# Block-sparse attention and a gated convolution feed-forward on one core: output turned on TensorE, one band exponential, gathers divided anew

## The chip, the cores and the metric

One core of one Trainium2 chip. The metric is the device time of one execution in microseconds. TensorE multiplies into PSUM; VectorE (DVE), ScalarE (ACT) and GpSimd (POOL) compute; SyncE (SP), ScalarE and POOL issue transfers. Each engine works through its own queue in order and waits on semaphores for the others.

## The reference

`q`, `k`, `v` have 4 batches, 8 heads, 768 positions and 64 channels. Blocks are of 32 positions, 24 in all. A query block sees its neighbours at distance at most 1, the first and the last block, and three sampled blocks from a table; the first and the last query block see everything.

```
scores = where(mask, q @ k.T / 8, -1e9);  attn = softmax(scores) @ v
x = attn with the heads side by side               # 4 x 768 x 512
h = relu(x @ w_in)                                 # 512 -> 1024
c = conv over positions, 3 taps per channel, of h
out = (h * sigmoid(c)) @ w_out                     # 1024 -> 512, float32
```

## The kernel before

**The planner.** The kernel does not issue its work in the order of the source. Each operation is entered with its engines and planned durations, its dependencies, the buffers that it takes or uses, and a due time; `Plan.run` (six passes and forty shaken trials) searches for an order of issue by list scheduling, and the instructions are then written out in that order, engine by engine. A planned duration or a dependency changes the order, never the data. The planner knows two transfer rings (POOL's, and one for all the others), a switch cost on TensorE, and buffers by pool. It knows nothing of how instructions reach an engine.

**The work.** There are 4 batches, 8 half-batches `n` (12 query blocks each), and in each of these 4 head pairs `hp`: 32 units of attention.
- Keys and queries: POOL loads a pair with a cast (L578), TensorE turns it (L606), ScalarE or VectorE evicts it as `kt` (L614, L616) and `qb` (L629, L631). POOL copies the keys of the first and last block into `kd` (L639, 64x64 tiles).
- Values: POOL loads half a batch (L656) into the one staging tile `vst`, POOL rearranges it (L669), SP writes it to a table `vs` in HBM (L677) and loads it back as `vn` (L684); POOL copies a version shifted by 64 rows (L692, two copies a batch), and SP loads the values of the first and last block as `vd` (L699, four small loads a batch).
- Sampled keys: VectorE copies 3 blocks for each of 11 query blocks out of `kt` at offsets read from registers (L740, 33 copies a half).
- Sampled values: the 11 blocks of a half are gathered out of `vs` into one of two `vg` buffers: `NIX` of them by indirect DMAs on POOL (L746; 4 in the first half, then 6), the others by SP with three transfers each (L755; in the first half three blocks by ScalarE).
- A unit of attention: band scores (L812, 11 matmuls), global scores (L841, L846), sampled scores (L864), each into one of two PSUM tiles `st`; the exponentials. That of the band is two instructions with a bias tile that holds -30000 in the rows outside the window (L821, 384 columns, and L822, 320 columns); the others are one each (L853, L871). A small memset zeroes one corner (L829, L831). The value product (L908, 67 matmuls) adds it all up, VectorE divides by the sum (L919, L920) into `xtok`, one of three, and SP turns that by a crossbar transpose into `xT` (L926).
- Feed-forward of a half: eight groups of four matmuls (L1062) that wait for the half's four `xT`, relu to `hE` (L1073 on ScalarE, L1075 on VectorE), then the convolution in four chunks of 256 channels. Chunks in `PEC` = (1, 3) run on TensorE with diagonal weights (L1023, six matmuls into an `st` tile); the others on VectorE (L976, six taps; L983, two adds). Then tanh (L991, L1032), a multiply (L1003, L1038), and the output product (L946), evicted (L954, L956) and stored by SP.

What sets the order around the change: the in-order queues of SP (value gathers, table writes, crossbar transposes, stores) and POOL (loads, copies, indirect gathers), the two `st` and four `mix` tiles of PSUM, and the planner's durations, such as `op({"POOL": 1.25}, ...)` for an indirect gather, `op({"DVE": 0.36}, cp, ...)` for three key copies and `op({"PE": 0.72}, a_fn, ...)` for a value product.

Of the kernel before, what the change touches and what calls it, by code (L numbers as in the profile page):

```python
# [52 lines left out]
class Op:  # L53
    __slots__ = ("alts", "fn", "prio", "deps", "lat", "dma", "mode", "allocs", "uses", "earliest", "outs",
                 "pend", "ready", "start", "end", "eng", "key", "done", "seq", "after", "lazy")
# [11 lines left out]
LAZY = 12.0  # L67


class Plan:  # L70
# [11 lines left out]
    def op(self, alts, fn, prio, deps=(), lat=None, dma=None, mode=None, alloc=(), uses=(), earliest=0.0,  # L82
           after=(), lazy=False):
        o = Op(alts, fn, prio, [d for d in deps if d is not None], lat, dma, mode, earliest)
        o.key = len(self.ops)
        o.lazy = lazy
        o.after = [d for d in after if d is not None]
# [22 lines left out]
    def forward(self, prio, first=True):  # L110
# [6 lines left out]
        rings = [0.0, 0.0]  # L117
        for o in ops:
# [12 lines left out]
        while left:  # L131
# [53 lines left out]
            if o.mode is not None:  # L185
                mode["PE"] = o.mode
            if o.dma is not None:
# [116 lines left out]
def kernel(  # L304
# [23 lines left out]
    PEC = (1, 3)  # L328
# [14 lines left out]
    NPA, NPR, NPG, NXK, NXT, NHE, NCV, NGT, NOS = 3, 3, 3, 3, 2, 2, 2, 2, 3  # L343
# [9 lines left out]
    vst = many(1, [96, 4, 8, 64], BF16, "vst")  # L353
# [20 lines left out]
    bias_f = sb.tile([128, 1], FP32, tag="bias_f", name="bias_f")  # L374
    bias_s = sb.tile([128, 1], FP32, tag="bias_s", name="bias_s")
# [17 lines left out]
    P_kg, P_vg, P_vn, P_vst, P_vr = pl.pool(NKG), pl.pool(NVG), pl.pool(NVN), pl.pool(1), pl.pool(1)  # L393
# [63 lines left out]
    def biases(e):  # L457
        nc.vector.memset(bias_f, 0.0)
        nc.vector.memset(bias_s, 0.0)
        nc.vector.memset(bias_f[96:128], -30000.0)  # L460
        nc.vector.memset(bias_s[0:32], -30000.0)
        nc.vector.memset(zrow, 0.0)
    bias_op = op({"DVE": 0.6}, biases, -7)
# [69 lines left out]
    for b in range(B):  # L533
        vs_zero.append(sp(lambda e, b=b: nc.sync.dma_start(out=vs_t[b][S:S + 32, :], in_=zrow), 4 + 8 * b, [bias_op],
                          0.1))
# [24 lines left out]
    def qk_load(P, x):  # L560
# [16 lines left out]
        else:  # L577
# [3 lines left out]
                after=[last_ld[0]], lazy=b > 0)  # L581
# [3 lines left out]
    def qk_pair(P):  # L585
# [9 lines left out]
        for x in range(2):  # L595
# [12 lines left out]
            trp = op({"PE": 0.42}, tr, due - 4 + 0.5 * x, [ld, i_sel, qm] + kt_w[b][:1], mode="T", alloc=[mb], uses=[nb])  # L608
            if x == 0:
# [7 lines left out]
                kt_w[b].append(op({"ACT": 0.70, "DVE": 0.62}, ev, due - 3, [trp] + kt_w[b][:1] + z_ops,  # L617
                                  uses=[mb, kt_buf[b]]))
                kev = kt_w[b][-1]
            else:  # L620
                qb_w[P] = []
                for h in range(2):
# [9 lines left out]
                    qb_w[P].append(op({"ACT": 0.70, "DVE": 0.62}, ev, due - 2.5, [trp, qm] + (qz[P:P + 1] if P < NQB else []),  # L632
# [15 lines left out]
    def v_batch(b):  # L648
        due = TS(8 * b)
        early = 0.0 if b == 0 else max(0.0, due - 26)  # L650
# [3 lines left out]
        for hf in range(2):  # L654
# [5 lines left out]
                dma=2.4, earliest=early, after=[last_v[0]], lazy=b > 0, uses=[] if nb else [he_first])  # L660
# [9 lines left out]
            alts = {"DVE": 0.75} if b == 0 else {"POOL": 2.3}  # L670
# [4 lines left out]
        for r in range(4):  # L675
# [8 lines left out]
        vn_w[b] = sp(lambda e: nc.sync.dma_start(  # L684
            out=VN[vn_buf[b].index], in_=vs_t[b][0:S].rearrange("(c p) e -> p c e", p=128)),
            due - 5, wr + [vm], 2.7, uses=[vn_buf[b]])
        vs_w[b] = []
        for h in range(2):
# [4 lines left out]
            vs_w[b].append(op({"DVE": 0.85} if b == 0 else {"POOL": 2.8}, sh, due - 3, [vn_w[b]], uses=[vn_buf[b]]))  # L693
        vd_w[b] = []
        for h in range(2):
            for x in range(2):
                def ldd(e, h=h, x=x):
                    rows = vs_t[b][(S - 32) * x:(S - 32) * x + 32, :].rearrange("p (a h d) -> p a h d", h=2, d=65)
                    nc.sync.dma_start(out=VD[vn_buf[b].index][64 * h + 32 * x:64 * h + 32 * x + 32, :,  # L699
                                                              65 * h:65 * h + 65], in_=rows[:, :, h, :])  # L700
# [451 lines left out]
```

## Time and profile before

| what | us |
|---|---|
| median of 3 runs | 319.02 |
| lowest, highest | 316.77, 325.29 |
| the profiled execution | 314.24 |
| its span from first to last instruction | 312.5 |

The profile is of one execution. Busy times are unions over an engine; a wait that names issue is time in which an engine waited for nothing that the profile shows. Line numbers are those of the kernel.

### The profile page before, as it was taken

What the parts mean: (1) busy time and instruction counts of PE and PEld (TensorE: products, weight loads), DVE (VectorE), ACT (ScalarE), POOL (GpSimd) and SP (SyncE); (2) the same over time, 40 slices, a digit from 0 to 9 for tenths busy, and PEclk for the clock granted to TensorE, in tenths of its full rate; (3) what the DMA queues carried; (4) which work ended last, traced back from release to release, by engine and by line L of the source; (5) the groups of instructions that cost most, each with busy time, mean ns of one, the idle gap of its engine ahead of it and who ended that gap; (6) DMA issues with size and microseconds to landing.
All of it is one profiled execution on the core that took longest, in us unless ns stands there. A gap on an engine that the chain in (4) does not pass through costs nothing.

```text
span 312.5 us, 10688 instructions
## 1 busy us (share of the span) xinstructions
PE 219.5 (70%) x4233; PEld 147.0 (47%) x4233; DVE 178.0 (57%) x652; ACT 162.0 (52%) x269; POOL 117.4 (38%) x170
## 2 busy tenths in 40 slices
PE   0744258659788293577895948997936577999994
PEld 0433147546445152366562635665624346676441
DVE  7725283027669682112685794744939246647781
ACT  2251255526557272336582853667823165966662
POOL 8157506910517388600066188305256600000000
PEclk9999999659999788958998697999985769999999
DMA  7987855990648924980379637965472431131013
GB/s 143 162 178 213 152 123 95 187 180 5 91 120 198 207 60 129 168 153 15 94 137 171 146 87 166 148 166 96 103 208 53 100 119 30 49 117 40 15 68 134
DMA packets 45542, 37.71 MB, mean 121 GB/s; under 512 B 19772, under 2 KB 40052, under 8 KB 45492
## 3 DMA queue, kind: packets, MB, share of 16 engines
q0 software_dynamic: 13216, 15.74, 29.5%
q1 hardware_dynamic: 31436, 20.59, 27.5%
q10 hardware_dynamic: 840, 0.70, 0.8%
q8 instruction: 33, 0.54, 0.8%
q14 instruction: 17, 0.14, 0.1%
HBM read 35.38 MB, written 9.62 MB: 144 GB/s over the span
## 4 chain that ended last, share of the span: by engine, by line
PE 46%; issue 14%; ACT 11%; DVE 10%; another core or an unknown queue 4%; DMA 2%; DVEq 1%; SPq 0%; ACTq 0%
PE mix L946 11%; PE mix L1062 11%; PE mix L908 9%; PE st L864 3%; DVE kg L740 3%; PE st L846 2%; ACT pr L871 2%; PE st L812 2%; PE st L1023 2%; PE mix L606 2%; ACT pg L853 2%; PE st L841 2%; ACT qb L629 2%; DMA vg<-vs 2%
## 5 line engine op out<-in xcount | busy, mean ns | idle before, releaser
L946 PE MATMUL mix<-woutb,gT 128*128 128x512 bf16 x192 | 53.6, 407 | 2.5 <-DVE gT L1038 1.2
L740 DVE COPY kg<-kt 128x128 bf16 x264 | 52.9, 241 | 3.7 <-issue 1.4
L746 POOL DMA_INDIRECT vg<-vs,idx x46 | 44.6, 969 | 22.9 <-issue 12.5
L1062 PE MATMUL mix<-xT,winb 128*128 128x384 bf16 x256 | 50.0, 345 | 1.7 <-DVE kt L616 1.3
L871 ACT ACTIVATE pr<-st 128x704 bf16<-128x704 f32 x32 | 24.2, 756 | 26.7 <-PE st L864 23.3
L812 PE MATMUL st<-qb,kt 128*128 128x64 bf16 x352 | 20.0, 210 | 23.7 <-issue 15.5
L853 ACT ACTIVATE pg<-st 128x736 bf16<-128x736 f32 x32 | 25.1, 785 | 21.5 <-PE st L846 9.9
L1062 PEld LDWEIGHTS <-winb 128*128 128x128 bf16 x256 | 25.5, 103 | 19.5 <-issue 6.0
L1073 ACT ACTIVATE hE<-mix 128x384 bf16<-128x384 f32 x53 | 25.8, 493 | 15.5 <-PE mix L1062 14.2
L908 PE MATMUL mix<-vg,pr 96*32 96x65 bf16 x704 | 28.4, 203 | 5.5 <-issue 5.5
L812 PEld LDWEIGHTS <-kt 128*128 128x128 bf16 x352 | 17.2, 109 | 28.7 <-issue 25.7
L606 PE MATMUL mix<-ident,nat 96*64 96x96 bf16 x512 | 18.4, 232 | 17.2 <-ACT kt L614 6.3
L578 POOL DMA_DIRECT2D nat<-in_k_dram x15 | 9.9, 665 | 54.4 <-PE mix L606 54.4
L908 PE MATMUL mix<-vn,pa 128*32 128x65 bf16 x384 | 25.5, 204 | 6.3 <-issue 6.3
L976 DVE TENSOR_SCALAR m<-hE,cw 128x384 bf16<-128x384 bf16 x96 | 23.7, 316 | 10.1 <-ACT hE L1073 10.1
L919 DVE RECIPROCAL rcp<-mix 128x6 f32<-128x6 f32 x32 | 6.2, 194 | 39.9 <-PE mix L908 39.8
L908 PE MATMUL mix<-vs,pa 128*32 128x65 bf16 x320 | 27.1, 203 | 2.6 <-issue 2.5
L908 PEld LDWEIGHTS <-pg 128*32 128x32 bf16 x736 | 23.5, 101 | 11.5 <-issue 11.4
L908 PE MATMUL mix<-vd,pg 128*32 128x130 bf16 x352 | 25.8, 234 | 2.8 <-issue 2.8
L908 PEld LDWEIGHTS <-pa 128*32 128x32 bf16 x704 | 22.0, 99 | 11.1 <-issue 10.8
L946 PEld LDWEIGHTS <-gT 128*128 128x128 bf16 x192 | 17.6, 103 | 19.9 <-issue 3.3
L864 PE MATMUL st<-qb,kg 128*128 128x64 bf16 x352 | 20.0, 210 | 9.1 <-ACT pa L822 6.2
(102 smaller groups left out, 433.7 us busy)
## 6 DMA issues: line engine op xcount, KB each, us to landing
out_dram<-o2s SPq DMA_DIRECT2D x24, 256.0 KB
vg<-vs SPq DMA_DIRECT2D x117, 32.5 KB
vn<-vs SPq DMA_DIRECT2D x4, 780.0 KB
nat<-in_k_dram POOLq DMA_DIRECT2D x15, 192.0 KB
nat<-in_q_dram POOLq DMA_DIRECT2D x15, 192.0 KB
vs<-vr SPq DMA_DIRECT2D x14, 195.0 KB
vst<-in_v_dram POOLq DMA_DIRECT2D x7, 384.0 KB
winb<-in_moe_w_in_dram POOLq DMA_DIRECT2D x1, 1024.0 KB
```

The lines of the kernel that those rows point to most:

```text
L606: nc.tensor.transpose(out=tp[64 * h:64 * h + 64, 96 * c:96 * c + 96], in_=nat[:, h, c, :], identity=ident[0:96, 0:96])
L740: nc.vector.tensor_copy(out=dst[:, :, x, 32 * s:32 * s + 32], in_=KT[kt_buf[b].index][:, :, bass.ds(block_off("DVE", i0 + x, s), 32)])
L746: vg_w[n].append(op({"POOL": 1.25}, lambda e, x=x: nc.gpsimd.indirect_dma_start(out=VG[vg_buf[n].index][:, x, :], out_offset=None, in_=vs_ ...
L812: nc.tensor.matmul(out=st[:, o + 64 * w:o + 64 * w + 64].rearrange("p (h s) -> p h s", h=2), lhsT=kt()[:, win(i):win(i) + 128], rhs=qcol(i ...
L853: nc.scalar.activation(out=pg_t[pg.index], in_=st_t[sg.index][:, 0:736], func=AF.Exp, bias=0.0, scale=0.125)
L864: nc.tensor.matmul(out=st[:, 64 * x:64 * x + 64].rearrange("p (h s) -> p h s", h=2), lhsT=kg[:, o:o + 128], rhs=qcol(i), start=True, stop= ...
L871: nc.scalar.activation(out=pr_t[pr.index], in_=st_t[sr.index][:, 0:704], func=AF.Exp, bias=0.0, scale=0.125)
L908: nc.tensor.matmul(out=dst, lhsT=l_, rhs=r_, start=(y == 0), stop=(y == len(lists[j]) - 1), skip_group_check=True)
L946: nc.tensor.matmul(out=mix_t[mb.index], lhsT=gT_t[gt_buf[n].index][:, ffc, 128 * c:128 * c + 128], rhs=woutb[:, ffc, :], start=(ffc == 0), ...
L976: nc.vector.tensor_scalar(out=mv(dst)[:, y], in0=hE_t[heb.index][:, f0 + y, c0 + tp_:c0 + tp_ + cn], scalar1=cw[:, tp_, f0 + y:f0 + y + 1] ...
L1062: nc.tensor.matmul(out=mix_t[hb.index][:, 0:384], lhsT=winb[:, fc, 128 * ffc:128 * ffc + 128], rhs=xT_t[xt_buf[n].index][:, fc, :], start= ...
L1073: nc.scalar.activation(out=dst, in_=src, func=AF.Relu, bias=0.0, scale=0.5)
```

## The change

- The output of a unit is turned by three TensorE transposes into a `mix` tile and evicted by ScalarE or VectorE into `xT`; the crossbar transposes go. `xtok` has two buffers and not three.
- The band is one exponential of 704 columns without a bias. The columns are ordered so that the blocks whose first 32 rows lie outside the window come first; these rows are zeroed by one memset of 32x384 behind the exponential (on VectorE or POOL), and the blocks at odd places multiply 96 rows, not 128.
- Indirect gathers: 4 in every half; the other 7 blocks by SP. Of the key copies 3 blocks in 11 (9 copies a half) go to POOL, with registers of its own.
- The convolution has one chunk on TensorE, `PEC` = (2,).
- The planner counts TensorE's instructions (`n`) and does not let an operation enter a page of 256 sooner than 2.3 us after the page before it was entered. Many planned durations are new.
- Values: staging in two buffers, no earliest time, rearranged by POOL or VectorE; `vn` loaded in halves; `vd` copied on the chip from `vn`. Two early query loads wait for writes of the value table; the weights are loaded in halves.

```diff
+PAGE, FETCH = 256, 2.3
...
+                        if o.n:
+                            g = (count + o.n) // PAGE
+                            if g != count // PAGE and s < pages.get(g, 0.0):
+                                s = pages[g]
...
+            if o.n:
+                g = (count + o.n) // PAGE
+                if g != count // PAGE:
+                    pages[g + 1] = o.end + FETCH
+                count += o.n
...
-    PEC = (1, 3)
+    PEC = (2,)
...
-    NPA, NPR, NPG, NXK, NXT, NHE, NCV, NGT, NOS = 3, 3, 3, 3, 2, 2, 2, 2, 3
+    NPA, NPR, NPG, NXK, NXT, NHE, NCV, NGT, NOS = 3, 3, 3, 2, 2, 2, 2, 2, 3
+    NVT = 2
...
-    vst = many(1, [96, 4, 8, 64], BF16, "vst")
+    vst = many(NVT, [96, 4, 8, 64], BF16, "vst")
...
-        early = 0.0 if b == 0 else max(0.0, due - 26)
+        early = 0.0
...
-                dma=2.4, earliest=early, after=[last_v[0]], lazy=b > 0, uses=[] if nb else [he_first])
+                dma=2.4, earliest=early, after=[last_v[0]], uses=[] if nb else [he_first])
...
-            alts = {"DVE": 0.75} if b == 0 else {"POOL": 2.3}
+            alts = {"DVE": 0.75} if b == 0 else {"POOL": 1.9, "DVE": 0.75}
...
-        vn_w[b] = sp(lambda e: nc.sync.dma_start(
-            out=VN[vn_buf[b].index], in_=vs_t[b][0:S].rearrange("(c p) e -> p c e", p=128)),
-            due - 5, wr + [vm], 2.7, uses=[vn_buf[b]])
+        vn_w[b] = []
+        for y in range(2):
+            vn_w[b].append(sp(lambda e, y=y: nc.sync.dma_start(
+                out=VN[vn_buf[b].index][:, 3 * y:3 * y + 3],
+                in_=vs_t[b][384 * y:384 * y + 384].rearrange("(c p) e -> p c e", p=128)),
+                due - 5, wr + [vm], 1.4, uses=[vn_buf[b]]))
...
-                    nc.sync.dma_start(out=VD[vn_buf[b].index][64 * h + 32 * x:64 * h + 32 * x + 32, :,
-                                                              65 * h:65 * h + 65], in_=rows[:, :, h, :])
-                vd_w[b].append(sp(ldd, due - 4.8, wr + [vm] + vz, 0.2, uses=[vn_buf[b]]))
+                    eng = nc.vector if e == "DVE" else nc.gpsimd
+                    src = VN[vn_buf[b].index][96 * x:96 * x + 32, 5 * x].rearrange("p (a h d) -> p a h d", h=2, d=65)
+                    r0 = 64 * h + 32 * x
+                    eng.tensor_copy(out=VD[vn_buf[b].index][r0:r0 + 32, :, 65 * h:65 * h + 65], in_=src[:, :, h, :])
+                vd_w[b].append(op({"DVE": 0.25, "POOL": 0.45}, ldd, due - 3, vn_w[b][x:x + 1] + vz, uses=[vn_buf[b]]))
...
-    NIX = [4] + [6] * (NHALF - 1)
+    NIX = [4] + [4] * (NHALF - 1)
...
+    KPX = 3
...
+            en = "POOL" if x >= NX - KPX else "DVE"
...
-            kg_w[n].append(op({"DVE": 0.36}, cp, due - 3 + 0.2 * x, [regs_d[g], km] + kt_w[b] + kgz,
+            kg_w[n].append(op({en: 0.55 if en == "DVE" else 0.95}, cp, due - 3 + 0.2 * x, [regs_p[g] if en == "POOL" else regs_d[g], km] + kt_w[b] + kgz,
                               uses=[kg_buf[n], kt_buf[b]]))
...
-            vg_w[n].append(op({en: 1.25}, gd, due - 3 + 0.5 * (x - NIX[n]), [regs_a if en == "ACT" else regs_s[g], vm]
+            vg_w[n].append(op({en: 1.75} if en == "SP" else {en: 2.1}, gd, due - 3 + 0.5 * (x - NIX[n]), [regs_a if en == "ACT" else regs_s[g], vm]
                               + vs_rows[b], dma=0.33, uses=[vg_buf[n]]))
...
-            nc.scalar.activation(out=p_[:, 0:384], in_=st[:, 0:384], func=AF.Exp, bias=b6, scale=0.125)
-            nc.scalar.activation(out=p_[:, 384:704], in_=st[:, 512:832], func=AF.Exp, bias=b5, scale=0.125)
-        ea = op({"ACT": t_act(384) + t_act(320)}, e_a, due, [so, bias_op], alloc=[pa], uses=[sa], lat=0.35)
+            nc.scalar.activation(out=pa_t[pa.index], in_=st_t[sa.index][:, 0:704], func=AF.Exp, bias=0.0, scale=0.125)
+        ea = op({"ACT": t_act(704)}, e_a, due, [so], alloc=[pa], uses=[sa], lat=0.35)
...
-            if g == 0:
-                eng.memset(p_[0:32, 0:64], 0.0)
-            else:
+            eng.memset(p_[0:32, 0:384], 0.0)
+            if g == 1:
                 eng.memset(p_[96:128, 320:384], 0.0)
-        fx = op({"POOL": 0.12, "DVE": 0.09}, fix, due + 0.5, [ea], uses=[pa])
+        fx = op({"DVE": 0.2 + 0.07 * g, "POOL": 0.45 + 0.1 * g}, fix, due + 0.5, [ea], uses=[pa])
...
-        xtr[(n, hp)] = sp(lambda e: nc.sync.dma_start_transpose(
-            out=xT_t[xt_buf[n].index][:, hp].rearrange("p (c s) -> p c s", c=3),
-            in_=xtok_t[xk.index].rearrange("p c h d -> p (c h d)")), due + 4.4, [no, xtr[(n, -1)]], 0.6, dur=1.27,
-            uses=[xk, xt_buf[n]])
+        xb = Buf(P_mix)
+
+        def xt(e):
+            tp = mix_t[xb.index].bitcast(BF16)
+            for c in range(3):
+                nc.tensor.transpose(out=tp[:, 128 * c:128 * c + 128],
+                                    in_=xtok_t[xk.index][:, c].rearrange("p h d -> p (h d)"), identity=ident)
+        xo = op({"PE": 0.19}, xt, due + 4.4, [no], mode="F", alloc=[xb], uses=[xk], n=6)
+
+        def xe(e):
+            src, dst = mix_t[xb.index].bitcast(BF16)[:, 0:384], xT_t[xt_buf[n].index][:, hp]
...
+        xtr[(n, hp)] = op({"ACT": 0.42, "DVE": 0.33}, xe, due + 4.8, [xo, xtr[(n, -1)]], uses=[xb, xt_buf[n]])
```

## Rows read from the trace of the kernel before

**Rows 1.** The page, part 1: busy us (share of the span) xinstructions.
```profile
PE 219.5 (70%) x4233; PEld 147.0 (47%) x4233; DVE 178.0 (57%) x652; ACT 162.0 (52%) x269; POOL 117.4 (38%) x170
```
**Rows 2.** Windows: length, busy us (x count) of PE, PEld, DVE, ACT, POOL; clock, DMA.
```profile
226.60:232.70 6.10, 1.28 (x7) 0.60 (x7) 1.88 (x11) 1.78 (x3) 3.74 (x5) 0.91 0.84 247
...
sum 37.10, PE 4.00 PEld 1.76 DVE 10.62 ACT 6.29 POOL 22.20; mean PE 0.67 PEld 0.29 DVE 1.77 ACT 1.05 POOL 3.70
```
**Rows 3.** Timeline of POOL: first and last of a train of six (start us, us).
```profile
163.11 1.19 POOL L746 DMA_INDIRECT vg<-vs,idx  x1 [0.30 <-issue]
...
169.69 0.92 POOL L746 DMA_INDIRECT vg<-vs,idx  x1 [0.30 <-issue]
```
**Rows 4.** Windows (columns as in rows 2), then SP's timeline, for one stretch.
```profile
42.70:53.10 10.40, 7.99 (x315) 6.92 (x318) 5.42 (x22) 7.33 (x13) 3.46 (x6) 1.00 0.38 64
...
42.73 10.38 SPq L755 DMA_DIRECT2D vg<-vs  x15
```
**Rows 5.** Queue of instructions (page, part 3), a window, pieces of the chain.
```profile
q8 instruction: 33, 0.54, 0.8%
...
66.20:134.30 68.10, 46.48 (x766) 29.22 (x766) 40.06 (x144) 34.86 (x57) 32.23 (x39) 0.88 0.64 131
...
57.09 2.22 issue
...
128.97 5.38 issue
...
261.85 1.68 issue
```
**Rows 6.** Waits of VectorE, the transposes (ns min/median/max), and TensorE's timeline late.
```profile
DVE xtok L920 <- DMA xT<-xtok: 10.0, 3, 7.7
...
L926 SPq DMA_TRANSPOSE xT<-xtok x32: 1179/1214/2016, 53.2 to 288.5; - x32
...
291.93 2.21 PE L1062 MATMUL mix<-xT,winb 128*128 128x384 bf16 x12
```
**Rows 7.** Groups (busy us, mean ns of one, idle before): exponentials and memsets.
```profile
L871 ACT ACTIVATE pr<-st 128x704 bf16<-128x704 f32 x32 | 24.2, 756 | 26.7 <-PE st L864 23.3 <-remote 1.8 <-issue 1.5
...
L821 ACT ACTIVATE pa<-st,bias_f 128x384 bf16<-128x384 f32 x16 | 9.3, 581 | 11.8 <-remote 5.9 <-PE mix L908 3.5 <-PE st L812 2.3
...
L822 ACT ACTIVATE pa<-st,bias_f 128x320 bf16<-128x320 f32 x16 | 8.4, 525 | 0.0
...
L829 DVE MEMSET pa<- 32x32 uint32 x12 | 1.0, 85 | 0.8 <-ACT pa L821 0.8
...
L462 DVE MEMSET xT<- 32x260 uint32 x1 | 0.3, 275 | 0.0
```
**Rows 8.** Groups: feed-forward eviction, taps, adds, convolution on TensorE.
```profile
L1073 ACT ACTIVATE hE<-mix 128x384 bf16<-128x384 f32 x53 | 25.8, 493 | 15.5 <-PE mix L1062 14.2 <-DVE gT L1003 0.6
...
L976 DVE TENSOR_SCALAR m<-hE,cw 128x384 bf16<-128x384 bf16 x96 | 23.7, 316 | 10.1 <-ACT hE L1073 10.1
...
L1023 PE MATMUL st<-hE,dg 128*128 128x384 bf16 x96 | 18.3, 326 | 0.1
...
L983 DVE TENSOR_TENSOR m<-m 128x768 bf16<-128x768 bf16 x32 | 17.7, 552 | 1.1 <-DVE gT L1100 0.9
```
**Rows 9.** Groups of copies, and timeline rows of VectorE beside POOL.
```profile
L740 DVE COPY kg<-kt 128x128 bf16 x264 | 52.9, 241 | 3.7 <-issue 1.4
...
L639 POOL COPY kd<-kt 64x64 bf16<-64x64 bf16 x32 | 8.2, 256 | 7.8 <-DMA vg<-vs,idx 6.0 <-ACT kt L614 0.6
...
180.73 4.85 POOL L692 COPY vs<-vn 64x2600 bf16<-64x2600 bf16 x2 [2.12 <-DMA vg<-vs,idx]
...
183.33 2.93 DVE L740 COPY kg<-kt 128x128 bf16 x6
```
**Rows 10.** Waits of POOL; the window of the last stretch.
```profile
POOL nat L578 <- PE mix L606: 54.6, 6, 25.9
...
280.00:312.50 32.50, 27.61 (x273) 15.06 (x261) 21.49 (x64) 16.70 (x29) 0.00 (x0) 1.00 0.20 64
```

More of the change, by code (lines that the diff above doesn't have):

```diff
@@ L54 @@
     __slots__ = ("alts", "fn", "prio", "deps", "lat", "dma", "mode", "allocs", "uses", "earliest", "outs",
-                 "pend", "ready", "start", "end", "eng", "key", "done", "seq", "after", "lazy")
+                 "pend", "ready", "start", "end", "eng", "key", "done", "seq", "after", "lazy", "n")
     def __init__(self, alts, fn, prio, deps, lat, dma, mode, earliest):
@@ L558, with qk_load @@
     nat_ld = {}
-    def qk_load(P, x):
+    def qk_load(P, x, behind=()):
         b, hp = divmod(P, 4)
@@ L580, in qk_load @@
                 (due - 9 if b else -5 + 2 * hp + x), alloc=[nb], dma=1.2, earliest=early,
-                after=[last_ld[0]], lazy=b > 0)
+                after=[last_ld[0]] + list(behind), lazy=b > 0)
             last_ld[0] = ld
@@ L767 @@
     gathers(1)
-    win_ld = op({"POOL": 0.85}, lambda e: nc.gpsimd.dma_start(
-        out=winb, in_=moe_w_in.rearrange("(fc p) ff -> p fc ff", p=128)), 12, dma=5.6, after=vg_w[0] + vs_w[0])
-    wout_ld = op({"POOL": 0.85}, lambda e: nc.gpsimd.dma_start(
-        out=woutb, in_=moe_w_out.rearrange("(ffc p) o -> p ffc o", p=128)), 24, dma=6.2, after=[win_ld] + vg_w[1])
-    last_v[0] = last_ld[0] = win_ld
+    win_ld, wout_ld = [], []
+    for y in range(2):
+        win_ld.append(op({"POOL": 0.85}, lambda e, y=y: nc.gpsimd.dma_start(
+            out=winb[:, :, 512 * y:512 * y + 512],
+            in_=moe_w_in.rearrange("(fc p) ff -> p fc ff", p=128)[:, :, 512 * y:512 * y + 512]), 12 + 2 * y, dma=3.0,
+            after=vg_w[0][:NIX[0]] + win_ld))
+    for y in range(2):
+        wout_ld.append(op({"POOL": 0.85}, lambda e, y=y: nc.gpsimd.dma_start(
+            out=woutb[:, 4 * y:4 * y + 4],
+            in_=moe_w_out.rearrange("(ffc p) o -> p ffc o", p=128)[:, 4 * y:4 * y + 4]), 24 + y, dma=3.2,
+            after=win_ld + vg_w[1] + wout_ld))
+    last_v[0] = last_ld[0] = win_ld[1]
     for b in range(1, B):
@@ L788, in attention @@
         due = TS(4 * n + hp)
-        odd = [1, 3, 5, 7, 9, 11] if g == 0 else [13, 15, 17, 19, 21]
-        even = [2, 4, 6, 8, 10] if g == 0 else [12, 14, 16, 18, 20, 22]
-        six, five = (odd, even) if g == 0 else (even, odd)
-        b6, b5 = (bias_f, bias_s) if g == 0 else (bias_s, bias_f)
         inner = list(range(1, 12)) if g == 0 else list(range(12, 23))
+        band = sorted(inner, key=lambda i: (i != 1 and i % 2, i))
         full = 0 if g == 0 else NB - 1
@@ L809, in s_a @@
             st = st_t[sa.index]
-            for o, lst in ((0, six), (512, five)):
-                for w, i in enumerate(lst):
-                    nc.tensor.matmul(out=st[:, o + 64 * w:o + 64 * w + 64].rearrange("p (h s) -> p h s", h=2),
-                                     lhsT=kt()[:, win(i):win(i) + 128], rhs=qcol(i), start=True, stop=True)
+            for w, i in enumerate(band):
+                nc.tensor.matmul(out=st[:, 64 * w:64 * w + 64].rearrange("p (h s) -> p h s", h=2),
+                                 lhsT=kt()[:, win(i):win(i) + 128], rhs=qcol(i), start=True, stop=True)
         so = op({"PE": 11 * 0.029}, s_a, due - 0.6, qb_w[P] + kt_w[b], mode="F", alloc=[sa],
-                uses=[kt_buf[b], qb_buf[P]], after=[prev_s])
+                uses=[kt_buf[b], qb_buf[P]], after=[prev_s], n=22)
         prev_s = so
         def e_a(e):
-            st = st_t[sa.index]
-            p_ = pa_t[pa.index]
-            nc.scalar.activation(out=p_[:, 0:384], in_=st[:, 0:384], func=AF.Exp, bias=b6, scale=0.125)
-            nc.scalar.activation(out=p_[:, 384:704], in_=st[:, 512:832], func=AF.Exp, bias=b5, scale=0.125)
-        ea = op({"ACT": t_act(384) + t_act(320)}, e_a, due, [so, bias_op], alloc=[pa], uses=[sa], lat=0.35)
+            nc.scalar.activation(out=pa_t[pa.index], in_=st_t[sa.index][:, 0:704], func=AF.Exp, bias=0.0, scale=0.125)
+        ea = op({"ACT": t_act(704)}, e_a, due, [so], alloc=[pa], uses=[sa], lat=0.35)
         def fix(e):
```

71 lines of the change are left out of this document (37 added, 34 removed).

## The prediction

> **What bounds the kernel now.** I read the busy shares first. TensorE is busiest, at 219.5 of 312.5 us, with VectorE at 57% and ScalarE at 52% [rows 1]: no engine is full, so the question is what the 93 idle us of TensorE are. Three views answer most of it.
>
> First, windows laid over the timeline's emptiest places. Six of them, 28.0 to 37.6, 101.4 to 107.6, 118.0 to 122.7, 167.2 to 172.0, 226.6 to 232.7 and 246.0 to 251.7, hold 37.1 us with 4.0 us of TensorE, 10.6 of VectorE and 6.3 of ScalarE, while POOL is busy for 22.2 [rows 2]. This is no wait of one engine for another, since all three stop. In each, POOL is in a train of indirect gathers: six at 1.32 us from start to start, the first at 163.11 [rows 3]. The stop begins about 3.7 us into a train (2.5 to 4.8) and ends about 1.4 us after its last gather; in 226.6 to 232.7 TensorE gets 7 matmuls out [rows 2]. SP issues value gathers in the same windows; but at 42.7 to 53.1 it issues 15 of them with no gather on POOL, and TensorE is busy for 8.0 of 10.4 us [rows 4]. So I read the stop as tied to the length of POOL's trains, not to SP's issues alone. Why the chip does this no row says.
>
> Second, the chain of waits has single pieces called issue of 1.3 to 5.4 us inside the value product L908 or between score groups. The six longest that lie outside those windows (57.09, 62.74, 128.97, 148.08, 210.53 and 261.85) sum to 16.0 us [rows 5]. Between such gaps TensorE executes whole multiples of 256 records: between the second and the third 766+766, six times 256 with four missing [rows 5]. The queue named instruction moved 33 packets in 0.54 MB, 16 KB each [rows 5], for the 8466 records of matmuls and weight loads [rows 1]: about 256 to a packet. These gaps are waits for code.
>
> Third, the remaining idle time: about 16 us of loading before 43 us, 4 us after the last matmul, some 24 us in small pieces.
>
> [...]
>
> **The change part by part.** The sum is made against the profiled execution, 314.24 us; the median of the runs shown, 319.02, stands 4.8 above it.
>
> *Gathers.* From the second half-batch on POOL issues 4 indirect gathers and not 6, so each train is shorter by 2 x 1.32 = 2.6 us, and the stop, which begins at the same place and ends with the train, by as much. In a stop TensorE still does 4.0/37.1 = 11% of a window's time, so one returns 2.3 us; six of them 14. Bounds: 0, if what stops the engines is all gathers together (their number stays 11 per half), and 33 (37.1 less 4.0), if trains of four never reach the place where the stop begins. I take 14, between them and by the rows' own geometry. SP gets 7 x 6 = 42 more issues; at 10.38/15 = 0.69 us each [rows 4] that is 29 us, against 32 transposes of 1.21 us, 39 us [rows 6], that it loses, and 16 small loads of the diagonal values.
>
> *Code blocks in the planner.* The plan now knows that a block of 256 must not be entered sooner than 2.3 us after the one before, and puts slower work between. It can return 0 to 16.0 us. Two of the six gaps are longer than 2.3 us by more than 1 us, where code arrives late, which the plan doesn't know: I take half, 8.
>
> *Attention output.* Thirty-two crossbar transposes go, each 1.2 us of SP's queue [rows 6] with value gathers and stores behind it. VectorE's 10.0 us of waiting for their buffers go too [rows 6]; they lie beside other TensorE work, hence 0, though the cover is thin (fewer output buffers, 2 and not 3). In the last half the transpose is issued at 288.5, and its reader starts at 291.93 [rows 6]; three TensorE transposes and an eviction take about 1.2 us in its place (0.33 and 0.49 by the rows of L1023 and L1073 [rows 8], and two handovers that I estimate at 0.2 each): minus 2. New: 96 transposes of 128 columns. No row has that form. The conv matmuls of 384 columns keep TensorE busy for 18.3/96 = 0.19 us each [rows 8]; a third of that is 64 ns: 6 us. Bounds: 6, if they run one into the other like those, and 31, at a whole duration of 326 ns; I take 6, since three stand together. New: 32 evictions of 128x384, 0.49 us by the ScalarE row of that shape [rows 8], half of that if the two-byte source is read faster: 8 to 16 us, on engines idle for over 40% of the span. I take 0 outside the last half.
>
> *One exponential.* 581+525 becomes about 756 ns [rows 7]: 0.35 us of ScalarE for each of 32, 11.2 in all. The value product now waits behind it for a memset of 32x384, between 85 and 275 ns on VectorE by its neighbours [rows 7], say 0.2; on POOL the same memset would queue behind gathers of 1.3 us each, and the value product, and the scores queued behind that on TensorE, behind it. Bounds of the two together: minus 11 to plus 6; I take minus 1, since ScalarE ends only a part of the chain.
>
> *Convolution.* One chunk in four, not two, stays on TensorE. TensorE loses 8 x 6 matmuls of 0.19 us, 9 us, against the 6 us of transposes: net minus 3, of which TensorE's 70% counts, minus 2. VectorE gains, for 8 chunks, six taps of 316 and two adds of 552 ns [rows 8], 3.0 us each, 24 us. In the last stretch, 280 to 312.5, VectorE is busy for 21.5 of 32.5 us [rows 10] and its taps stand between the last matmuls: plus 3 there in full. The other seven chunks, 21 us, fall where VectorE has room (idle for 43% of the span [rows 1]): I take a fifth, plus 4; bounds 0 and 21.
>
> *Key gathers.* Three blocks of eleven go to POOL: 72 of VectorE's 264 copies of 241 ns [rows 9], 17 us less. On POOL one should cost what its copies of small tiles do, 0.26 us (the 64x64 diagonal copy), up to the 0.49 that a colliding VectorE copy takes (below): 18 to 35 us, against 14 gathers of about 1 us [rows 3] that go. The row against it: while POOL copies the shifted values at 180.73 for 4.85 us, VectorE needs 2.93 us for six key copies [rows 9], 0.49 us each. Cost 0 in the sum, since VectorE gets 17 us back; the collision is in the rival below.
>
> *Values earlier.* Value loads are no longer held back, have two buffers and may be rearranged on VectorE. POOL waited 54.6 us in 6 waits in front of key and query loads [rows 10], with the value rearrangement queued behind them. Bounds 0 and minus 8 (a third of the small pieces); I take minus 4. The diagonal values come from on-chip copies: 16 small ones, beside others, 0. The weight loads in halves: 0.
>
> Sum: -14 -8 -2 -1 -2 +3 +4 -4 = -24. 314.2 - 24 = 290 for a profiled execution, and 295 on the scale of the median.
>
> **The rivals.**
> (a) *The stops go altogether.* For: their onset lies after three gathers, and POOL's key copies may split a train of four. Against: 118.0 to 122.7 began only 3.2 us into its train, before a fourth ended. The term becomes 33: 295 - 19 = 276.
> (b) *The gathers' split does nothing*: the stops stay as long, because they hang on gathers in flight from POOL and SP together. For: SP's issues are in every stop. Against: 42.7 to 53.1 [rows 4]. 295 + 14 = 309.
> (c) *VectorE paces the feed-forward; slower.* Place: the stretches after each half's first matmuls. VectorE gets 3.0 us of taps and adds per half, four evictions (up to 0.49 each) and four memsets (0.2), 5.8 us; 8 halves, 46 us, against the 17 us of key copies saved elsewhere. Each POOL copy beside a VectorE copy adds up to 0.25 us (0.49 less 0.24 [rows 9]), 72 of them 18. That is 64 us, of which the sum has 7 on the chain. It decides where half of them are: 32 in place of 7 gives 320, two thirds, 43, give 331; the case's price is 326. For: VectorE is two thirds busy in the last stretch. Against: 43% idle overall.
> [...]
>
> **How the numbers follow.** Forecast 0.50, with an own range of 282 to 307 (gathers 7 to 20, code 3 to 13); (a) 0.14; (b) 0.20; (c) 0.16. Within 2% of 319, about what a measurement tells from no change, is 312.6 to 325.4. Faster by over 2%: nearly all of the forecast, all of (a), half of (b), 0.70. Within: half of (b), a fifth of (c) and a little of the forecast, 0.16. Slower: most of (c), 0.14. The range of 8 in 10 runs from 272, just under (a), to 320, just under (c)'s low end.
>
> **What would show it.** Right: all-engine stops of some 3 us per train and about 20 us in sum; TensorE's issue gaps at multiples of 256 records halved; no xT transposes on SP, first matmuls of a half starting about 1.2 us after its last output; one band exponential of some 756 ns. Wrong: stops of 5 us behind trains of four (b), none (a), or taps and adds with over 10% of the chain and VectorE above 75% busy (c).

## The result and the profile after

The changed kernel took 277.8 us (median of 3 runs, 273.81 to 279.69) where the kernel before took 319.02: a ratio of .868, with an interval of .838 to .898. The forecast was 295.0 with a range of 272 to 320, so direction and range hold and the point is 17 us too high. The profiled execution of those three (279.69 us) was a slow one, 2.1% above the fastest (273.81), so the lines below are from the same kernel profiled again (278.22 us, span 276.5; experiment 1).

Busy shares and the shares of the chain that ended last (parts 1 and 4 of the page) of the changed kernel; the last line has part 1 of its first profile:

```profile
PE 206.0 (75%) x4264; PEld 144.5 (52%) x4281; DVE 198.6 (72%) x661; ACT 158.5 (57%) x251; POOL 136.0 (49%) x253
...
PE 49%; DVE 21%; DMA 10%; issue 9%; ACT 4%; DVEq 2%; SPq 1%; another core or an unknown queue 1%; POOL 0%; ACTq 0%; POOLq 0%
...
PE 212.0 (76%) x4281; PEld 146.3 (53%) x4281; DVE 198.2 (71%) x661; ACT 158.5 (57%) x251; POOL 137.4 (49%) x253
```

The profile of experiment 1 lacks 17 matmul records (4264 beside 4281 weight loads), 16 of them of the output product, some 0.4 us each: its TensorE is busy for about 6 us more than it says. So [rows 1], where none is missing, is compared with the first profile, where none is missing either: the time in which TensorE does nothing fell from 312.5 - 219.5 = 93.0 to 277.9 - 212.0 = 65.9 us, and its busy time by 7.5. VectorE rose from 57% to 72%, under the 75% that I had named as a sign of rival (c); its taps and adds have 8% of the chain, where I had named 10%. The next fence has the groups that answer to [rows 6 to 9]: line, engine, operation and shapes, count, then busy us and mean ns of one, then the idle time before.

```profile
L1005 DVE TENSOR_SCALAR m<-hE,cw 128x384 bf16<-128x384 bf16 x144 | 41.3, 354 | 1.5 <-ACT hE L1102 1.5
L754 DVE COPY kg<-kt 128x128 bf16 x192 | 34.7, 243 | 1.7 <-POOL kd L644 0.7 <-issue 0.4
...
L838 ACT ACTIVATE pa<-st 128x704 bf16<-128x704 f32 x32 | 24.2, 756 | 21.1 <-PE st L831 13.2 <-remote 3.5 <-PE st L861 3.0
L754 POOL COPY kg<-kt 128x128 bf16 x72 | 20.1, 321 | 0.7 <-ACT kt L619 0.2
...
L1052 PE MATMUL st<-hE,dg 128*128 128x384 bf16 x48 | 10.1, 350 | 0.0
L948 PE MATMUL mix<-ident,xtok 128*128 128x128 bf16 x96 | 10.1, 226 | 2.5 <-DVE xtok L937 2.5
...
L844 POOL MEMSET pa<- 32x384 bf16 x21 | 9.5, 454 | 54.0 <-ACT pa L838 53.7
L955 ACT COPY xT<-mix 128x384 bf16<-128x384 bf16 x20 | 9.2, 479 | 17.7 <-PE mix L948 13.9 <-issue 3.6 <-remote 0.3
...
L957 DVE COPY xT<-mix 128x384 bf16<-128x384 bf16 x12 | 4.2, 354 | 10.3 <-PE mix L948 7.6 <-remote 2.8
...
L844 DVE MEMSET pa<- 32x192 uint32 x11 | 2.4, 218 | 1.9 <-ACT pa L838 1.4 <-issue 0.4
```

The durations I had worked out for single operations were near: one band exponential 756 ns as forecast, a transpose 226 ns (10.1 us in all, between my 6 and 31), an eviction 479 or 354 ns (forecast 490 at most), a memset 218 ns on VectorE (0.2 us), a key copy on POOL 321 ns (260 to 490). The miss does not lie in these. A tap of the convolution is the exception, 354 ns for the 316 of [rows 8]. Its median (the middle one of least, median, most, in ns) is 311; the mean is raised by a few that run beside POOL's copies of the shifted values:

```profile
L1005 DVE TENSOR_SCALAR m<-hE,cw x144: 300/311/2489, 53.7 to 266.2; 128x384 bf16<-128x384 bf16 x144
...
87.98 6.39 DVE L1005 TENSOR_SCALAR m<-hE,cw 128x384 bf16<-128x384 bf16 x6
...
88.61 2.35 POOL L700 COPY vs<-vn 64x2600 bf16<-64x2600 bf16 x1
...
91.90 2.35 POOL L700 COPY vs<-vn 64x2600 bf16<-64x2600 bf16 x1
...
96.56 0.63 PE L975 MATMUL mix<-woutb,gT 128*128 128x512 bf16 x1 [6.60 <-DVE gT L1067]
```

Two of these six taps take 2.49 and 2.47 us, each over the whole of a POOL copy, and TensorE waits 6.60 us for what follows them, its longest stop in this trace behind the loading at the start. That is a collision of the kind that rival (c) priced; in the third chip's trace of this kernel (experiment 10) no tap takes over 0.53 us.

The stops are the first thing to look for. In the trace of before, six windows lost 37.1 - 4.0 = 33.1 us of TensorE [rows 2]. Outside the loading at the start, the changed kernel has four stretches in which all three engines do little beside gathers, in windows of the kind of [rows 2]:

```profile
40.30:45.20 4.90, 2.03 (x67) 1.52 (x54) 0.36 (x1) 1.51 (x2) 4.28 (x6) 0.85 1.19 242
105.60:110.70 5.10, 2.43 (x85) 2.08 (x81) 1.27 (x4) 0.24 (x1) 2.61 (x4) 0.80 0.98 201
156.30:160.10 3.80, 1.20 (x25) 0.60 (x24) 0.60 (x6) 1.84 (x3) 2.87 (x4) 0.96 0.68 149
218.00:221.60 3.60, 1.42 (x15) 0.88 (x15) 1.30 (x5) 0.80 (x2) 2.05 (x3) 1.00 0.65 193
sum 17.40, PE 7.07 PEld 5.08 DVE 3.54 ACT 4.38 POOL 11.81; mean PE 1.77 PEld 1.27 DVE 0.88 ACT 1.10 POOL 2.95
```

They lose 17.40 - 7.07 = 10.3 us, where I had named some 20 as the sign of a right forecast, and TensorE works for 41% of them, where it was 11%. In the second, 2.67 us are a gap at a multiple of 256 records, of the kind of [rows 5] (called the code kind below; experiment 3). Of the eight trains of four two stand whole, from 38.52 and from 75.68, and only the first has a stop behind it; two more (from 20.88 and 128.01) have a memset or two between. The gathers of the other halves lie apart, at 106.59, 107.88 and then 116.38, 117.67, or at 186.41, 193.20, 194.56 and 197.55, with other work and waits of POOL between.

### The profile page after: what moved, and what is told of

It is laid out like the page before. It is cut to its first block, busy times and chain, and to the rows that moved or that the text cites. A ratio compares the mean times of both kernels' runs of the same rounds, so it can differ in the third digit from the quotient of the medians.

```text
span 277.9 us, 10957 instructions
## 1 busy us (share of the span) xinstructions
PE 212.0 (76%) x4281; PEld 146.3 (53%) x4281; DVE 198.2 (71%) x661; ACT 158.5 (57%) x251; POOL 137.4 (49%) x253
## 4 chain that ended last, share of the span: by engine, by line
PE 45%; DVE 18%; issue 13%; DMA 7%; ACT 5%; POOL 3%; DVEq 2%; SPq 1%; ACTq 1%; another core or an unknown queue 0%; POOLq 0%
PE mix L1091 11%; PE mix L925 10%; PE mix L975 7%; DVE kg L754 4%; DVE m L1005 3%; PE st L831 3%; PE st L879 3%; DMA vg<-vs 3%; PE st L861 3%; DMA vs<-vr 2%; DVE m L1012 2%; DMA vg<-vs,idx 2%; PE mix L611 2%; DVEq L754 2%; PE st L856 2%
## 5 line engine op out<-in xcount | busy, mean ns | idle before, releaser
L975 PE MATMUL mix<-woutb,gT 128*128 128x512 bf16 x192 | 50.2, 392 | 12.2 <-DVE gT L1032 6.6
L1005 DVE TENSOR_SCALAR m<-hE,cw 128x384 bf16<-128x384 bf16 x144 | 39.1, 339 | 3.3 <-ACT hE L1102 3.2
L754 DVE COPY kg<-kt 128x128 bf16 x192 | 39.0, 270 | 1.6 <-POOL kd L644 0.7
L760 POOL DMA_INDIRECT vg<-vs,idx x32 | 33.2, 1037 | 9.2 <-issue 8.3
L925 PE MATMUL mix<-vs,pa 128*32 128x65 bf16 (+1 forms) x320 | 29.3, 202 | 8.0 <-issue 7.6
L975 PEld LDWEIGHTS <-gT 128*128 128x128 bf16 x192 | 17.5, 99 | 30.2 <-DVE gT L1032 8.2
L868 ACT ACTIVATE pg<-st 128x736 bf16<-128x736 f32 x32 | 25.1, 784 | 13.4 <-PE st L861 9.0
L838 ACT ACTIVATE pa<-st 128x704 bf16<-128x704 f32 x32 | 24.2, 756 | 14.6 <-PE st L831 11.9
L1012 DVE TENSOR_TENSOR m<-m 128x768 bf16<-128x768 bf16 x48 | 27.7, 595 | 0.0
L925 PEld LDWEIGHTS <-pr 96*32 96x32 bf16 x704 | 24.6, 100 | 4.3 <-issue 3.5
L925 PE MATMUL mix<-vn,pa 96*32 96x65 bf16 (+1 forms) x384 | 25.9, 203 | 0.5 <-issue 0.5
L925 PEld LDWEIGHTS <-pa 128*32 128x32 bf16 (+1 forms) x704 | 22.3, 99 | 6.8 <-issue 6.4
L1020 ACT ACTIVATE m<-m 128x768 bf16<-128x768 bf16 x24 | 19.8, 847 | 9.1 <-DVE m L1012 8.8
## 6 DMA issues: line engine op xcount, KB each, us to landing
vg<-vs SPq DMA_DIRECT2D x159, 32.5 KB
```

The source lines that it names most:

```text
L754: eng.tensor_copy(out=dst[:, :, x, 32 * s:32 * s + 32], in_=KT[kt_buf[b].index][:, :, bass.ds(block_off(e, i0 + x, s), 32)])
L760: vg_w[n].append(op({"POOL": 1.25}, lambda e, x=x: nc.gpsimd.indirect_dma_start(out=VG[vg_buf[n].index][:, x, :], out_offset=None, in_=vs_ ...
L838: nc.scalar.activation(out=pa_t[pa.index], in_=st_t[sa.index][:, 0:704], func=AF.Exp, bias=0.0, scale=0.125)
L868: nc.scalar.activation(out=pg_t[pg.index], in_=st_t[sg.index][:, 0:736], func=AF.Exp, bias=0.0, scale=0.125)
L925: nc.tensor.matmul(out=dst, lhsT=l_, rhs=r_, start=(y == 0), stop=(y == len(lists[j]) - 1), skip_group_check=True)
L975: nc.tensor.matmul(out=mix_t[mb.index], lhsT=gT_t[gt_buf[n].index][:, ffc, 128 * c:128 * c + 128], rhs=woutb[:, ffc, :], start=(ffc == 0), ...
```

## The experiments

They ran in three groups, each on one chip: 1 to 4 on the first (before: 322.77 us, 319.79 to 323.63), 5 to 8 on the second (before: 291.42, 283.52 to 293.86), 9 to 12 on the third (before: 289.88, 284.86 to 294.41). Times are compared within a group. An edit of one line makes the planner write a new order for the whole kernel, so each experiment changes its part and the order with it; two such edits, 3 and 11, ended within 1.1 us of their controls. That the kernel before takes 30 us less on two of the chips is a finding of its own (experiment 9).

**1. The changed kernel again**, for its profile and as the control of the first group.

> The changed kernel once more, as the yardstick on this chip: 274 to 280 us, a ratio to the kernel before of 0.84 to 0.90. If it lay above 0.90, the gain measured first would be in part the state of the kernel before.

277.89 us (277.52 to 279.88), ratio .864 [.857, .871]: 44.9 us less than before. Its profile is the one above.

**2 and 4. The gathers' split alone**, undone in the changed kernel and done alone in the kernel before.

```
-    NIX = [4] + [4] * (NHALF - 1)      (changed kernel)
+    NIX = [4] + [6] * (NHALF - 1)
-    NIX = [4] + [6] * (NHALF - 1)      (kernel before)
+    NIX = [4] + [4] * (NHALF - 1)
```

> The changed kernel with six indirect gathers on POOL again in every half but the first, all else as changed. Theory T (the stops of all engines hang on the length of POOL's trains): trains of six bring back 2.3 to 2.6 us of stop in each of seven halves, 16 to 18 us, so 291 to 296 us. Rival R (stops hang on all gathers in flight, whoever issues them): within 4 us of the changed kernel. Rival S (the planner's new order does it, trains or not): within 4 us as well, but then the stops in the timeline are no longer than in the changed kernel although the trains are.

> The kernel before with four indirect gathers on POOL in every half, nothing else changed. Theory T: stops shorter by 2.3 to 2.6 us in six or seven halves, 14 to 18 us: 301 to 305 us against 319. If trains of four never reach the stop's beginning: 33 us less, 286. Rival R: 315 to 322 us.

Undone: 294.77 us (293.97 to 295.41), 16.9 above the control. Done alone: 298.8 (297.69 to 301.75), 24.0 below before, ratio .927 [.920, .934]. My term was 14, with bounds 0 and 33. On this chip the split is worth 17 to 24 us, the largest single part measured here, and rival (b) falls. How it costs differs from what I had said, though: the time of experiment 2 is that of theory T, but not its stops. No train of six stands whole in that run, and four stretches behind its gathers, laid as those of the control, lose 18.00 - 9.47 = 8.5 us, no more than the control's 10.3. The last two of them, and the sum:

```profile
113.00:119.10 6.10, 2.91 (x116) 2.31 (x104) 0.56 (x3) 0.98 (x2) 5.42 (x8) 0.88 0.62 158
208.90:213.40 4.50, 2.09 (x52) 1.63 (x53) 0.49 (x2) 1.12 (x3) 2.70 (x5) 0.97 0.28 70
sum 18.00, PE 9.47 PEld 7.21 DVE 1.92 ACT 3.84 POOL 14.87; mean PE 2.37 PEld 1.80 DVE 0.48 ACT 0.96 POOL 3.72
```

Part 1 and the clock row of the page with six on POOL in the changed kernel:

```profile
PE 216.9 (74%) x4264; PEld 148.5 (51%) x4281; DVE 196.7 (67%) x670; ACT 163.7 (56%) x259; POOL 137.4 (47%) x250
...
PEclk9955586995999859799987998889979799979998
```

Against the control, with the same number of matmul records, TensorE's idle time is 293.6 - 216.9 = 76.7 us, 6.2 more than the control's 70.5, and its busy time 10.9 more: the mean of L975 goes from 396 to 409 ns, of the value product's 96x65 form from 200 to 205, and the mean granted clock is .869 for .925 (three early slices stand at 5 tenths, behind two in which TensorE is busy for 0 and 6 tenths; the control has one). So only about a third of the 17 us is idle time, and none of it shows as stops behind trains. A lower clock alone does not carry the rest: experiment 3 has .87 too, with TensorE busy for 210.9 us, 4.9 of the 10.9 more, at the control's time. What makes up the rest of the 17 us these runs do not settle.

**3. The planner's code rule off** in the changed kernel.

```
-PAGE, FETCH = 256, 2.3
+PAGE, FETCH = 256, 0.0
```

> The changed kernel with the planner's code rule off (the time for a block of code set to 0), all else as changed, the planned durations too. If the rule returns what was forecast, 8 us: 284 to 288 us and issue gaps of TensorE at multiples of 256 records that sum to 16 us or more instead of about 10. If code fetch is hidden, or the rule is of no use: within 4 us, and gaps that sum to about 10 us.

277.43 us (275.39 to 278.06) against 277.89: the rule is worth nothing that these runs show, where I had 8. Gaps at multiples of 256 records are still there [rows 5]: these are the two longest of them among the chain's pieces called issue, first of the control, then without the rule.

```profile
60.22 1.88 issue
...
106.06 2.67 issue
```

```profile
107.84 2.63 issue
...
183.54 2.25 issue
```

I also summed TensorE's issue gaps that lie at the same place of each 256 instructions. (Matmuls, weight loads and the queue's own instructions are counted, and a missing matmul record by its weight load: the gaps then stand behind some 193 or 194 of each 256.) The sums are 17.1 us in the trace of before, 21.1 in experiment 4, 9.4 in the control and 9.9 without the rule. So they shrank to about half in the changed kernel, as I had named for a sign, but not through the rule. What goes with them is the crossbar: in the five traces that have its transposes they sum to 13.6 to 21.1 us (17.1, 21.1, and experiments 5, 9 and 12 with 17.4, 13.6 and 15.7), in the nine without them to 8.9 to 13.4, and on each of the three chips of the experiments the runs with it lie above those without. Each is one trace, and how the one acts on the other no run shows.

**5 to 8. One part each undone**, in the changed kernel, on the second chip: the crossbar for the attention output (with its third buffer), two convolution chunks on TensorE, all key gathers on VectorE, the old durations in the plan.

```
-        xo = op({"PE": 0.19}, xt, ...)
-        xtr[(n, hp)] = op({"ACT": 0.42, "DVE": 0.33}, xe, ...)
+        xtr[(n, hp)] = sp(lambda e: nc.sync.dma_start_transpose(...), ..., dur=1.27, uses=[xk, xt_buf[n]])
-    PEC = (2,)
+    PEC = (1, 3)
-    KPX = 3
+    KPX = 0
-            vg_w[n].append(op({en: 1.75} if en == "SP" else {en: 2.1}, gd, ...
+            vg_w[n].append(op({en: 1.25}, gd, ...
```

(The last pair stands for eight such lines.)

> The changed kernel with the output turned by the crossbar again (and three output buffers), all else as changed. By my sum (transposes worth 2 us, TensorE's own transposes a small cost): 276 to 282 us. Theory Q (the rest of the gain is SP's queue: 32 transposes of 1.2 us in front of value gathers, and their small packets in front of code and data): 288 to 298 us, issue gaps at multiples of 256 records back to 15 us or more.

> The changed kernel with two convolution chunks on TensorE, as before. By my sum (the third chunk on VectorE costs 3 in the last stretch and 4 elsewhere, and frees 3 on TensorE): 271 to 276 us, faster than the changed kernel. Theory V (VectorE has room for it and the freed score tiles of PSUM are worth more): 280 to 288 us.

> The changed kernel with all key copies on VectorE. By my sum (moving them was worth nothing): 276 to 280 us. Theory V' (VectorE is now the engine that key copies delay, 71% busy): 282 to 290 us. If POOL's copies block VectorE's, as the rival (c) had it: 270 to 275 us.

> The changed kernel planned with the durations of before (gathers by SP 1.25, three key copies 0.36, register loads 0.22, the evictions, copies and the value product as before), no operation changed. By my sum, in which the durations have no term: 276 to 280 us. Theory D (the rest of the gain is the better plan): 288 to 298 us.

Crossbar 273.92 us (272.09 to 279.12), two chunks 265.07 (260.69 to 266.64), keys on VectorE 270.34 (267.8 to 273.04), old durations 272.22 (267.11 to 273.03), where before was 291.42. The changed kernel itself was not in this group, so none of the four had its control. Hence the third group.

**9. The kernel before, with a profile,** on the third chip.

> The kernel before, again, with a profile on the chip of this call. Earlier the same kernel took 319 to 323 us on two chips and 291 us on a third, and there the profiles of four variants of the changed kernel had only 2 to 4 us of TensorE issuing one by one behind gather trains, where the other chip's had 10 to 17. Theory T (the stop behind POOL's gather trains depends on the chip): if the time is near 291 the six windows of [rows 2] lose under 15 us in sum, where they lost 33; if it is near 320 they lose 30 or more. Rival (the 28 us between chips lie in the loading at the start, or in the granted clock): the six windows lose 30 us or more also at 291.

289.79 us (287.74 to 292.94). After five of its trains of six I laid windows from 3.7 us behind a train's first gather to 2.7 behind the start of its last, here and in the trace of before. First the sum in the trace of before, then this run's windows.

```profile
sum 27.40, PE 5.11 PEld 3.21 DVE 7.82 ACT 3.67 POOL 16.17; mean PE 1.02 PEld 0.64 DVE 1.56 ACT 0.73 POOL 3.23
```

```profile
101.80:107.20 5.40, 3.45 (x41) 2.32 (x43) 4.90 (x26) 3.31 (x5) 2.79 (x3) 0.75 1.13 262
118.60:124.10 5.50, 1.93 (x99) 1.63 (x94) 1.54 (x5) 0.53 (x1) 4.54 (x5) 1.00 0.47 131
160.20:165.80 5.60, 3.56 (x62) 2.38 (x55) 5.14 (x29) 3.69 (x6) 3.14 (x5) 1.00 1.15 246
...
sum 27.20, PE 16.89 PEld 12.41 DVE 20.43 ACT 13.78 POOL 16.25; mean PE 3.38 PEld 2.48 DVE 4.09 ACT 2.76 POOL 3.25
```

POOL is as busy (16.25 and 16.17 us), with the same trains of six. But TensorE works for 16.89 us of 27.20, where it was 5.11 of 27.40, and VectorE for 20.43, where it was 7.82. One train of the five still stops all three (118.6 to 124.1). So the loss behind trains goes from 22.3 to 10.3 us with no change of the kernel: the stop is not a fixed price of a train of gathers, but depends on the chip or on what that chip was under. The whole difference of this kernel between the two profiles is 312.5 - 289.8 = 22.7 us, of which these windows hold 12 and the gaps of the code kind 17.1 - 13.6 = 3.5.

**10. The changed kernel on the same chip,** the control.

> The changed kernel beside the kernel before on the same chip. Theory T: where before is near 291, the change is worth 45 less the 17 to 24 us of the stops, so 21 to 28 us: 263 to 270; where before is near 320, again 275 to 280. Rival (the gain does not depend on the stops): a ratio of .86 on any chip, so 251 at 291.

265.15 us (261.43 to 272.67), 24.7 below before, ratio .918 [.911, .925]. On a chip where the stops are mostly absent the change gains 25 us and not 45, inside the 263 to 270 that the theory gave; a ratio of .86 everywhere is out. The 20 us between the two gains are about what the split alone is worth on the first chip (16.9 and 24.0); that the split is what is missing is argued from this, since it was not run alone on the third chip.

**11. Two chunks on TensorE again.**

> Two convolution chunks of four on TensorE in the changed kernel, now beside the changed kernel itself. By my sum the move of the chunk to VectorE costs 7 and returns 2, so undoing it is 5 us faster than the changed kernel (2 to 8). Rival: the move pays (VectorE has room, TensorE is the bound), and undoing it is 2 us or more slower.

266.21 us (261.19 to 271.31), 1.1 above the control with ranges that cover each other: no difference. I had 5 us faster, so neither my price of the added VectorE work nor the rival's gain shows. VectorE does 182.3 us of work for the control's 193.6, TensorE 204.6 for 201.2, and the time stays.

**12. The crossbar again.**

> The attention output again turned by the crossbar on SP, all else as changed, beside the changed kernel. My sum gave the transposes on TensorE 2 us at the end and 6 us of TensorE against it, a net of about 0 to 4 us slower with the crossbar back. Rival 1: the crossbar's 39 us of SP's queue, in front of value gathers that now are twice as many per half on SP, cost far more: 8 us or more slower. Rival 2: the 96 transposes and 32 evictions cost more than the crossbar's queue: 2 us or more faster.

275.25 us (272.65 to 277.79), 10.1 above the control; ratios to before .958 [.952, .965] and .918 [.911, .925]. That is rival 1 by its time, and the second chip agrees: there it lies 8.9 above the two-chunk kernel, here 9.0. Where the 10 us arise the traces show only in part. With the crossbar back, the timeline of SP's queue over the first two halves (start and length in us, operation), and then the same stretch of the control:

```profile
24.68 19.27 SPq L769 DMA_DIRECT2D vg<-vs  x21
44.14 1.33 SPq L943 DMA_TRANSPOSE xT<-xtok  x1
45.72 2.20 SPq L769 DMA_DIRECT2D vg<-vs  x3
48.73 1.19 SPq L943 DMA_TRANSPOSE xT<-xtok  x1
50.16 3.90 SPq L769 DMA_DIRECT2D vg<-vs  x6
54.11 16.56 SPq L943 DMA_TRANSPOSE xT<-xtok  x5
```

```profile
23.30 23.10 SPq L769 DMA_DIRECT2D vg<-vs  x30
```

The 30 gathers are out at 46.4 us without the crossbar and at 54.1 with it: SP stands in front of a transpose until the output it turns is there. Over the run it waits 55.9 us in 28 waits at L943. The largest of them, of SP's queue:

```profile
SPq L943 <- DVE xtok L937: 25.8, 7, 9.1
```

These waits are no proof of the cost, though. In the control SP waits as long elsewhere, 125.2 us in all for 112.1 with the crossbar, most of it in front of stores and table writes. The first unit's output is already later with the crossbar, before its first transpose is issued at 44.14; of these lines the first is with the crossbar:

```profile
43.55 0.56 DVE L937 TENSOR_TENSOR xtok<-mix,rcp 128x384 bf16<-128x384 f32 x1
```

```profile
36.90 0.56 DVE L937 TENSOR_TENSOR xtok<-mix,rcp 128x384 bf16<-128x384 f32 x1
```

Experiment 5's trace agrees in both, with 43.39 and the gathers out at 54.2. The gaps of the code kind sum to 15.7 us for the control's 12.6. TensorE's longest stop with the crossbar is not the crossbar's: it is for a key copy on POOL behind a copy of the shifted values that takes 6.44 us, for 2.35 elsewhere in this trace, and in experiment 5's trace it is 2.38 and no such stop is there:

```profile
99.85 6.44 POOL L700 COPY vs<-vn 64x2600 bf16<-64x2600 bf16 x1 [4.01 <-DMA vg<-vs,idx]
...
106.70 0.24 PE L879 MATMUL st<-qb,kg 128*128 128x64 bf16 x1 [7.78 <-POOL kg L754]
```

So it is shown that the crossbar, with the order that the planner makes for it, costs 10 us; that SP's queue is the place of it is argued.

The first matmuls of a half also come later. In the last half, the output's last instruction, what turns it, and the feed-forward that reads it: the crossbar first, then TensorE.

```profile
251.70 0.56 DVE L937 TENSOR_TENSOR xtok<-mix,rcp 128x384 bf16<-128x384 f32 x1
...
256.25 2.93 PE L1079 MATMUL mix<-xT,winb 128*128 128x384 bf16 x17
```

```profile
235.48 0.56 DVE L937 TENSOR_TENSOR xtok<-mix,rcp 128x384 bf16<-128x384 f32 x1
...
236.07 0.49 PE L948 MATMUL mix<-ident,xtok 128*128 128x128 bf16 x6
236.43 0.86 ACT L955 COPY xT<-mix 128x384 bf16<-128x384 bf16 x2 [0.65 <-PE mix L948]
...
237.54 2.76 PE L1091 MATMUL mix<-xT,winb 128*128 128x384 bf16 x16
```

From the output's end to the matmuls it is 256.25 - 252.26 = 4.0 us by the crossbar and 237.54 - 236.04 = 1.5 by TensorE, a gain of 2.5 here.

The third group also gives the second its missing scale. The crossbar and the two-chunk kernel ran in both, at 273.92 and 275.25, and at 265.07 and 266.21: each 1.1 to 1.3 us apart. Taking that off the control gives an estimate of 264 for the changed kernel on the second chip. By it keys on VectorE cost 6 us and the old durations 8, both less certain than the rest, since their ranges (267.1 to 273.04) meet the control's (261.43 to 272.67); by the lower runs alone (267.8 and 267.9, and a single 267.11, beside 261.43 to 263.84) both cost about 5.

## Why the prediction came out as it did

The likeliest case had the right direction and, for the time, ended nearer to rival (a) (276). By its terms:

*Gathers, 14 us.* Right in kind and too small on the first chip: 17 to 24. The step that failed is "the stop begins at the same place and ends with the train": trains of four are not six less two. Of the two that stand whole one has a stop from 1.8 us into the train, and the other none. The windows' loss falls from 33.1 to 10.3 us, in part because POOL's other work stands between gathers, nearer to rival (a); but undoing the split brings back 17 us with no more of such stops, so the windows do not account for the term. And the term is no constant: on the third chip the stops to be won were mostly absent (10.3 us behind five trains of six, for 22.3).

*Code blocks, 8 us: 0.* I took the gaps as what the rule returns. The step that failed is "I take half": gaps of up to 2.67 us stay in the chain with the rule, and without it they are no worse (9.9 us for 9.4). (The six gaps of 16.0 us were those at the place of 256, not the six longest: 242.50 has 1.51.) They did shrink, with the crossbar's transposes gone, which my sum had not linked. In the control's trace 6 of some 33 such places, one in each 256, show a gap of over half a microsecond, 9.4 us in sum; that agrees with a rule that is worth nothing.

*Attention output, 2 us, and nothing elsewhere: 10 us.* The step that failed is "beside other TensorE work, hence 0". The last half returns 2.5 us, where I had 2.0 (the matmuls start 1.5 us after the output, for 1.2). The rest lies in the other halves. I had set SP's 29 added us of issues against 39 that go, as busy time, and had no term for a transpose that stands in SP's queue, in front of value gathers, and waits for its input, nor for the gaps of the code kind, 3.1 us more with the crossbar on the third chip. How the 10 us divide between these and the plan's new order stays open. After the split SP has 7 blocks of gathers in a half where it had 5, so the expectation's "twice as many" is too much.

*Convolution, plus 7 less 2: 0.* The estimate that a fifth of VectorE's added work counts was too high. In the last 32.5 us VectorE is busy for 23.7 us, for 21.5 in [rows 10], and two chunks or one on TensorE makes no difference. The price of rival (c) falls with it: VectorE is at 72%, its taps and adds at 8% of the chain. Its collision does occur, at 6.6 us of TensorE's waiting in the control of the first chip.

*Key gathers, 0: some 5 to 6 us in favour.* The row that I had set against the move, VectorE's key copies beside a POOL copy of the shifted values [rows 9], is no single case: in the first chip's control VectorE's key copies take 191 ns (107 of them) with POOL not computing, 270 (55) beside POOL's key copies and 379 (30) beside its other work, one of them 2.34 us beside a copy of the shifted values. That the mean is 243 ns, for 241 in [rows 9], hides it: before the change 237 took 200 and 27 beside POOL's work 600. So the move does not cost, but not because the engines leave each other alone.

*Plan durations, not priced at all: some 5 to 8 us.* I read the corrected numbers as no work of their own. They set the order that the plan writes, and the estimate from experiment 8 is near the term that I gave to the code rule: that the one too much and the other too little nearly cancel is luck. *Values earlier* (4) and *one exponential* (1) were not tried alone. POOL's wait before key and query loads did fall, from 54.6 us [rows 10] to 15.4. Against the exponential stands the memset that I had feared on POOL: in experiment 10 TensorE waits 4.2 us at 187.65 for one that stands behind a copy of the shifted values.

On the third chip, the crossbar's 10, the keys' 5 to 6 and the durations' 5 to 8 would make 20 to 24 of the 24.7 us. They need not add up, and two of them are estimates; I take the agreement as no proof. On the first chip the split's 17 to 24 come on top.

## What to carry to other kernels

A queue's cost is not its busy time: taking 32 transposes out of SP's queue was worth 10 us where their issue time was made good by other issues, so try such a removal alone before it is priced at nothing. A mean over a group can hide a collision (243 ns for the key copies, one of which takes 2.34 us): look at the longest of a group beside its median. A loss that a trace shows beside a train of transfers should be measured on more than one chip before it is priced (here 22.3 us on one and 10.3 on another), and each group of variants needs its control on the same chip. Gaps that a trace shows are not what a rule against them returns (here 9.4 us with the rule and 9.9 without); try the rule alone. Before gaps are summed by their place in a count of records, see whether the trace has all the records.

## What was not expected of the hardware

The same kernel ran at 322.77 us on one chip and at 289.88 and 291.42 on two others, with the same gathers in the same trains. The part of it that the windows show is how far TensorE, VectorE and ScalarE go on behind a train of six indirect gathers (TensorE is busy for 19% of the windows in the first measurement, at 319.02, and for 62% on the third chip). What differs between the chips no run shows, and why the engines stop is open as it was. On the chip with the stops, the run with six gathers on POOL also has TensorE busy for 10.9 us more at the same number of matmul records, with a mean granted clock of .869 for .925; 4.9 us of that come without the six gathers too, in experiment 3 at .870. The gaps at one place of each 256 of TensorE's instructions were longer in every trace with crossbar transposes (13.6 to 21.1 us) than in any without (8.9 to 13.4). And VectorE and POOL held each other up in both directions: taps of 2.49 us for a median of 0.31, and a POOL copy of 6.44 us for 2.35 (what held that one is inferred from VectorE's copies and taps beside it).
